# Copying a finished accumulator behind its last product, and wider planned spacing between engines, in a fused attention and feed-forward kernel

## Chip, core and metric

One core of one Trainium2 chip. The metric is the device time of one execution in microseconds (us), as a median over runs. The engines named below are TensorE (PE, its weight loads PEld), VectorE (DVE), ScalarE (ACT), GpSimd (POOL, here mostly an issuer of transfers) and SyncE (SP, the issuer of the other transfers). Each engine takes its instructions strictly in the order in which the program gives them to it.

## The reference

```python
# q, k, v: (4, 12480, 128); agents: (4, 49, 128); w_in: (128, 2048); w_out: (2048, 128)
def sm(a, b):
    s = scale * (a @ b.transpose(0, 2, 1))
    s = s - s.max(-1, keepdims=True)
    e = np.exp(s)
    return e / (e.sum(-1, keepdims=True) + 1e-09)
a2k = sm(agents, k)
agent_v = a2k @ v
q2a = sm(q, agents)
x = (q2a @ agent_v).reshape(49920, 128)
h = x @ w_in
g = np.maximum(h, 0.0) ** 2
out = g @ w_out
```

## The kernel before

The 49,920 rows are worked in 52 groups (`NSG`) of 960 rows (`ST`), 13 groups to each of the 4 batches. A group passes through 16 blocks (`NF`), one for each 128 columns of the 2048 wide hidden layer, so there are 832 blocks (`NG`). Products in float32 are made from a high part, rounded to the short format that TensorE takes, and a low part, the rest; each product is then three products.

A block `i` has these steps. `mm1(i)` (L493) makes 128 x 960 hidden values from the group's softmax rows `p_a` (high) and `p_b` (low) and the folded weights `w_a`, `w_b`: six matmuls, two at a time in the two halves of the array. `relu(i)` (L497) and `square(i)` (L500) run on ScalarE. `high(i)` rounds to `gh`, on VectorE (L507) for odd blocks and by a transfer issued from GpSimd (L505) for even ones. `low(i)` (L511) makes `gl` on VectorE. `mm2(i)` (L527) adds the block to the group's output, which fills the two accumulator banks `out0` and `out1`: twelve matmuls, eight blocks (`LAG`) behind `mm1`.

The two banks of `out` exist once (`ps_o`, `bufs=1`). When the last `mm2` of a group has run, `store_a` (L540) copies `out0` on ScalarE and `store_d` (L544) copies `out1` on VectorE into `ob`, and one transfer on SyncE's queue (L546) sends `ob` out. The first `mm2` of the next group overwrites the banks, and waits for both copies.

Beside that runs the attention work of later groups. For the softmax rows of a group the steps are `q_load`, `q_scores` (PE, L408), `q_turn` (DVE, L416), `q_shift` (DVE), `q_exp` (ACT, L432), `q_share` (DVE, from L436), `q_back` (DVE, L453), `q_spread` (eight small transfers on SyncE's queue, L461), `q_hi` (ACT, the cast that makes `p_a`, L465) and `q_lo` (DVE, which makes `p_b`, L468). The keys and values of the next batch are worked in similar chains (`k_pair`, `kp_copy`, `kp_max`, `k_exp`, `k_hi`, `v_hi`, `v_lo`, `v_acc`), which share one accumulator tile (`ps_att`, one buffer) with the query scores.

The order of everything is written by a planner. `at(t, f, ...)` files a step under a number `t` whose whole part is the block during which it is to run, a slot; all steps are sorted by `t` and issued in that order to their engines. In slot `i`, `mm2` of the pair that is due comes at `i`, `mm1(i)` at `i + .01`, `relu(i)` at `i + .1` (or `.035`), `square(i-1)` at `i + .2`, `low(i-4)` (odd) at `i + 0`, `low(i-5)` (even) at `i - .1`, `high(i-2)` at `i + .35`, and one step of the attention chains for each engine at `i + .5`. `chain` finds free slots for a chain: from a step on one engine to the next on another it leaves the number of slots in the table `hop`, and a bank's slots are held in `banks`. Slots of the copies are in `taken`, and the two or three slots up to them in `kept`, which only the steps in `urgent` may use.

The slot in which a group's last `mm2` runs is called T below: `T = s*16 + 23` for group `s`. There, `mm1(T)` and (by `early_mm1`, in all groups but the last three) `mm1(T+1)` are issued between the last `mm2` of the group and the first of the next, with `q_scores` of a later group ahead of them.

Of the kernel before, what the change touches and what calls it, by code (L numbers as in the profile page):

```python
# [9 lines left out]
F32 = mybir.dt.float32  # L10
# [7 lines left out]
P = 128  # L18
CH = 120
G = 8  # L20
TT = CH * G // 2
ST = CH * G
# [3 lines left out]
def agent_attention_relu2_kernel(ctx: ExitStack, tc: tile.TileContext, qT, kT, v, agT, w_in, w_out, outT):  # L26
# [6 lines left out]
    nc = tc.nc  # L33
    C, B, NCH, _ = kT.shape
# [11 lines left out]
    wk = ctx.enter_context(tc.tile_pool(name="wk", bufs=2))  # L46
# [424 lines left out]
    NSG = B * NS  # L471
# [3 lines left out]
    outs = {}  # L475
# [60 lines left out]
    obs = {}  # L536

    def store_a(s):
        obs[s] = wk.tile([P, 2, TT], F32, name="ob", bufs=1)
        nc.scalar.copy(obs[s][:, 0, :], outs[s][0][:, :TT])  # L540

    def store_d(s):
        ob = obs.pop(s)
        nc.vector.tensor_copy(ob[:, 1, :], outs.pop(s)[1][:, :TT])  # L544
        if s < NSG - 1:
            nc.sync.dma_start(out=outT[:, s * ST:(s + 1) * ST], in_=ob.rearrange("p t n -> p (t n)"))  # L546
        else:
            for t in range(2):
                nc.sync.dma_start(out=outT[:, s * ST + t * TT:s * ST + (t + 1) * TT], in_=ob[:, t, :])


    LAG = 8
    TAIL, EARLY = 52, 8
# [3 lines left out]
    def by_dma(i):  # L557
        return i % 2 == 0 and FROM <= i < NG - 4
# [4 lines left out]
    def at(t, f, *args):  # L563
        steps.append((t, len(steps), f, args))

    hop = {"PE": {"PE": 1, "PX": 0, "ACT": 0, "DVE": 0}, "PX": {"ACT": 0}, "ACT": {"PE": 2, "ACT": 1, "DVE": 0, "POOL": 3},
           "DVE": {"PE": 2, "ACT": 1, "DVE": 1, "POOL": 3}, "POOL": {"PE": 1, "ACT": 4, "DVE": 4, "POOL": 1}}
    taken = {(e, s * NF + NF - 1 + LAG) for s in range(NSG) for e in ("ACT", "DVE")}  # L570
    kept = {(e, s * NF + NF - 1 + LAG - x) for s in range(NSG) for e, n in (("ACT", 3), ("DVE", 2)) for x in range(n)}
    taken |= {("PE", s * NF + NF - 1 + LAG) for s in range(NSG - 3)}
# [2 lines left out]
    def chain(t, todo):  # L575

        first = prev = None
        while todo:  # L580
            n = 1
            while todo[0][0] == "PE" and n < len(todo) and (todo[n][1] in reads_bank and todo[n][0] != "PE" or todo[n][1:-1] == todo[n - 1][1:-1] and todo[n][1] is not k_max):
                n += 1
            t += hop[prev][todo[0][0]] if prev else 0
            while True:
                g, p, ts = t, None, []
                for e, f, *_ in todo[:n]:
                    g += hop[p][e] if p else 0
                    while (e, g) in taken or f not in urgent and (e, g) in kept:
                        g += 1  # L590
                    ts.append(g)
                    p = e
                held = range(ts[0], ts[-1] + (3 if todo[0][1] is v_acc else 2)) if todo[0][0] == "PE" else ()
                if not any(y in banks for y in held):
                    break
                t += 1
            banks.update(held)
            for (e, f, *args), g in zip(todo, ts):
                taken.add((e, g))
                at(g + (.005 + .015 * args[2] if f is w_make and args[2] < 2 else .5), f, *args)  # L600
            first = ts[0] if first is None else first
            prev, t, todo = p, ts[-1], todo[n:]
        return first, t
# [4 lines left out]
    def plan_queries(s):  # L608

        t = (s - 3) * NF + NF - 1 + LAG  # L610
        g = t + 1
        while ("DVE", g) in taken:
            g += 1
        banks.update(range(t, g + 2))
        taken.add(("DVE", g))
        at(t - 6, q_load, s)
        at(t + .005, q_scores, s)
        at(g + .5, q_turn, s)
        plan_rows(s, g + 1)

    def plan_rows(s, g):
        _, t = chain(g, [("DVE", q_shift, s), ("ACT", q_exp, s), ("DVE", q_share, s), ("DVE", q_back, s)])
        at(t + .9, q_spread, s)
        _, t = chain(t + 5, [("ACT", q_hi, s), ("DVE", q_lo, s)])
        assert t + 2 < s * NF, (s, t)

    def plan_queries_early(s, base):
        first, t = chain(base, [("PE", q_scores, s), ("DVE", q_turn, s)])
        plan_rows(s, t + 1)
        at(first - 6, q_load, s)  # L630
# [53 lines left out]
    order, t = {}, 6.3  # L684
# [37 lines left out]
    for n in range(NS):  # L722
        t = order["k", n] + 1.7
# [7 lines left out]
    for n in range(NS):  # L731
        t = t1 if n == 0 else max(t1 + .6 * n, order["v", n - 1] - .5) if n < S1 else t2 if n == S1 else order["v", n - 2] + .6
# [4 lines left out]
    t = order["q", 0] + .9  # L737
# [3 lines left out]
    for n in range(7):  # L741
        t = (10.3, 15.6, 27, 31.2, 35, 46, 52)[n]
# [5 lines left out]
    t = last  # L748
# [16 lines left out]
    at(3.08, q_scores, 1)  # L765
    at(4.04, q_turn, 1)
    banks.update([*range(5), *(x + y for x in SKIP for y in range(3))])
    plan_rows(1, 5)
    taken.update((e, t) for e in ("ACT", "DVE") for x in SKIP for t in (x, x + 1))
    for n in range(AHEAD, EARLY):  # L770
        at(3.55 + 2 * (n - AHEAD), k_load, 1, n)
# [16 lines left out]
    early_mm1 = {s * NF + NF + LAG + x: s * NF + NF - 1 + LAG + x + .02 for s in range(NSG - 3) for x in range(2)}  # L788
    for i in range(NG):
        late = i in SKIP or i < NF + LAG and (i < LAG or (i - LAG) % NF == 0)  # L790
        at(early_mm1.get(i, i if late else i + .01), mm1, i)
        at(i + (.035 if i + 1 in early_mm1 and i not in early_mm1 else .1), relu, i)
        at(i + 1.2, square, i)
        if i < FROM:
            at(i + 1.35, high, i)
            at(i + (2.32 if i <= SKIP[0] else 3.3), low, i)
        elif by_dma(i):
            at(i + 3.05, high, i)
            at(i + 4.9, low, i)
        else:  # L800
            at(i + 2.35, high, i)
            at(i + 4, low, i)
    for i in range(NF + LAG):
        j = i - LAG + sum(i <= x for x in SKIP)
        if j >= 0 and i not in SKIP:
# [5 lines left out]
                at(j + LAG + x + .001 * y, mm2, j + y, x ^ (j // 2 % 2), x + y + j % NF == 0, x + y == 2 and j % NF == NF - 2)  # L811
    for s in range(NSG - 1):
        t = s * NF + NF - 1 + LAG
        at(t + (.08 if t + 1 in early_mm1 else .15), store_a, s)
        at(t + .25, store_d, s)
    t, way = NG, (NG - LAG) // 2 % 2
    for js in (range(NG - LAG, NG - LAG // 2), range(NG - LAG // 2, NG)):
        for x in range(2):
            for j in js:
                at(t, mm2, j, way ^ x, False, x == 1 and j == NG - 1)  # L820
                t += 1
        way ^= 1
    at(t + .1, store_a, NSG - 1)
    at(t + .2, store_d, NSG - 1)
    with tc.manual_schedule():
        for _, _, f, args in sorted(steps, key=lambda x: x[:2]):
# [25 lines left out]
```

## Time and profile before

| | us |
|---|---|
| median of 3 runs | 1961.61 (1957.45 to 1962.17) |
| the profiled execution, its own time | 1961.79 |
| span of the profiled execution, first to last instruction | 1960.0 |
| TensorE busy (matmuls / weight loads) | 1847.1 / 1621.3 |
| ScalarE busy | 1663.2 |
| VectorE busy | 1598.2 |

The profiled execution's time lies within 0.2 us of the median, so sums made against its span can be read as sums against the median. Busy times of matmuls overlap, since one starts before the last has ended; where TensorE stood still is read from the starts of its instructions. An idle time is printed in brackets behind the instruction that ended it, with what it had waited for.

### The profile page before, as it was taken

What the parts mean: (1) busy time and instruction counts of PE and PEld (TensorE: products, weight loads), DVE (VectorE), ACT (ScalarE), POOL (GpSimd) and SP (SyncE); (2) the same over time, 40 slices, a digit from 0 to 9 for tenths busy, and PEclk for the clock granted to TensorE, in tenths of its full rate; (3) what the DMA queues carried; (4) which work ended last, traced back from release to release, by engine and by line L of the source; (5) the groups of instructions that cost most, each with busy time, mean ns of one, the idle gap of its engine ahead of it and who ended that gap; (6) DMA issues with size and microseconds to landing.
All of it is one profiled execution on the core that took longest, in us unless ns stands there. A gap on an engine that the chain in (4) does not pass through costs nothing.

```text
span 1960.0 us, 45341 instructions
## 1 busy us (share of the span) xinstructions
PE 1847.1 (94%) x18297; PEld 1621.3 (83%) x18297; DVE 1598.2 (82%) x2131; ACT 1663.2 (85%) x2015; POOL 325.3 (17%) x501
## 2 busy tenths in 40 slices
PE   9999999999999999999999999999999999999998
PEld 8688779888888887888887888877888788888887
DVE  6677888888888887888888888987887877888786
ACT  3578879888888988898888889987998898989897
POOL 0011122121111111122112213111111111111110
PEclk9999989999999999999999999999999999999999
DMA  9354544555444554554444454544444444444442
GB/s 342 121 169 143 197 155 163 190 184 186 155 156 168 167 185 168 170 192 156 164 170 141 168 168 166 179 158 148 163 157 146 143 159 151 158 161 157 161 148 102
DMA packets 110323, 325.19 MB, mean 166 GB/s; under 512 B 16672, under 2 KB 30368, under 8 KB 110112
## 3 DMA queue, kind: packets, MB, share of 16 engines
q0 software_dynamic: 58752, 200.57, 28.8%
q1 hardware_dynamic: 51360, 121.72, 18.8%
q8 instruction: 143, 2.34, 0.5%
q14 instruction: 68, 0.56, 0.1%
HBM read 83.35 MB, written 25.56 MB: 56 GB/s over the span
## 4 chain that ended last, share of the span: by engine, by line
PE 47%; DVE 20%; issue 10%; ACT 10%; DMA 8%; SPq 5%; ACTq 0%; DVEq 0%; POOLq 0%
PE out L527 27%; DVE gl L511 12%; PE h L493 12%; SPq L461 5%; DMA gh<-g 4%; ACT g L500 3%; DMA pt<-et 3%; ACT g L497 3%; DVE gh L507 3%; PE ps_att L192 3%; PE out L302 1%; PE ps_att L408 1%; PE ps_att L281 1%; DVE ob L544 1%; DVE sm L436 1%
## 5 line engine op out<-in xcount | busy, mean ns | idle before, releaser
L511 DVE TENSOR_TENSOR gl<-g,gh 128x960 fp32r<-128x960 f32 x832 | 934.5, 1158 | 100.3 <-PE out L527 69.8
L497 ACT ACTIVATE g<-h 128x960 f32<-128x960 f32 x832 | 814.0, 978 | 181.1 <-PE h L493 180.1
L500 ACT ACTIVATE g<-g 128x960 f32<-128x960 f32 x832 | 842.3, 1013 | 0.0
L527 PE MATMUL out<-gh,wo_hi 64*128 64x480 f32 x3328 | 728.8, 376 | 70.2 <-ACT ob L540 50.5
L527 PE MATMUL out<-gl,wo_hi 64*128 64x480 f32 x3328 | 713.6, 371 | 7.8 <-DVE gl L511 6.1
L527 PE MATMUL out<-gh,wo_lo 64*128 64x480 f32 x3328 | 711.8, 368 | 0.0
L527 PEld LDWEIGHTS out<-gh,wo_hi 64*128 64x128 f32 x3328 | 400.7, 188 | 121.2 <-ACT ob L540 69.6
L505 POOL DMA_DIRECT2D gh<-g x408 | 226.9, 556 | 1497.6 <-PE h L493 465.2
L527 PEld LDWEIGHTS out<-gl,wo_hi 64*128 64x128 f32 x3328 | 401.9, 188 | 49.5 <-DVE gl L511 26.6
L527 PEld LDWEIGHTS out<-gh,wo_lo 64*128 64x128 f32 x3328 | 404.7, 190 | 21.3
L493 PE MATMUL h<-p_a,w_a 49*128 49x480 f32 x1664 | 358.1, 382 | 16.5 <-ACT g L497 16.2
L493 PE MATMUL h<-p_a,w_b 49*128 49x480 f32 x1664 | 343.9, 365 | 0.0
L493 PE MATMUL h<-p_b,w_a 49*128 49x480 f32 x1664 | 343.8, 365 | 0.0
L507 DVE CAST gh<-g 128x960 fp32r<-128x960 f32 x424 | 285.4, 673 | 5.5 <-ACT g L500 4.7
L493 PEld LDWEIGHTS h<-p_a,w_a 49*128 49x128 f32 x1664 | 193.9, 188 | 59.0 <-ACT g L497 33.1
L493 PEld LDWEIGHTS h<-p_b,w_a 49*128 49x128 f32 x1664 | 195.8, 190 | 10.2
L493 PEld LDWEIGHTS h<-p_a,w_b 49*128 49x128 f32 x1664 | 192.2, 186 | 11.9
L468 DVE TENSOR_TENSOR p_b<-pt,p_a 113x480 fp32r<-113x480 f32 x52 | 34.3, 659 | 91.0 <-ACT p_a L465 82.6
L436 DVE TENSOR_REDUCE sm<-e 128x8 f32<-128x392 f32 x52 | 29.1, 560 | 95.7 <-ACT e L432 95.7
L251 POOL TENSOR_TENSOR sk<-sk,mM 120x196 f32<-120x196 f32 x78 | 91.8, 1187 | 15.9 <-PE ps_att L192 11.5
L192 PEld LDWEIGHTS ps_att<-ag_sb,kt 64*120 64x120 f32 x1248 | 77.1, 185 | 5.3 <-issue 2.8
L465 ACT CAST p_a<-pt 113x480 fp32r<-113x480 f32 x52 | 30.8, 593 | 57.2 <-DMA pt<-et 46.8
(127 smaller groups left out, 994.2 us busy)
## 6 DMA issues: line engine op xcount, KB each, us to landing
gh<-g POOLq DMA_DIRECT2D x408, 480.0 KB, 3.1
vt<-v SPq DMA_DIRECT2D x52, 516.0 KB, 5.4
qt<-qT SPq DMA_DIRECT2D x52, 488.0 KB, 4.4
kt<-kT SPq DMA_DIRECT2D x52, 480.0 KB, 5.8
outT<-ob SPq DMA_DIRECT2D x51, 480.0 KB, 2.6
pt<-et SPq DMA_DIRECT2D x416, 30.0 KB, 2.4
raw<-w_in SPq DMA_DIRECT2D x4, 512.0 KB, 7.8
raw<-w_out SPq DMA_DIRECT2D x4, 512.0 KB, 6.3
```

What stands on the lines that cost most here:

```text
L192: mm = nc.tensor.matmul(ps[:CH, u, r * A:(r + 1) * A], cols[u][r][rows], ag_sb[rows, b, :A], start=x == 0 and r == 0, stop=x == 1 and r == ...
L251: eng.tensor_tensor(out=x, in0=x, in1=m.rearrange("p (o a) -> p o a", o=1).to_broadcast([CH, G if h is None else H, A]), op=ALU.subtract)
L436: nc.vector.tensor_reduce(out=sms[s], in_=es[s][:, :, :A], axis=AX.X, op=ALU.add)
L461: nc.sync.dma_start(out=pts[s][to:to + 32, j % 2 * QW:(j % 2 + 1) * QW], in_=src[32 * j:32 * j + 32, h, :QW])
L468: nc.vector.tensor_tensor(PT[s][1][:M], pts.pop(s)[:M], PT[s][0][:M].bitcast(F32), op=ALU.subtract)
L493: nc.tensor.matmul(hs[i][:, t, :TT], w, two(p), start=n == 0, stop=n == 2)
L497: nc.scalar.activation(gs[i], hs.pop(i)[:, :, :TT], AF.Relu)
L500: nc.scalar.activation(gs[i], gs[i], AF.Square)
L505: nc.gpsimd.dma_start(out=ghs[i], in_=gs[i])
L507: nc.vector.tensor_copy(ghs[i], gs[i])
L511: nc.vector.tensor_tensor(out=gls[i], in0=gs.pop(i), in1=ghs[i].bitcast(F32), op=ALU.subtract)
L527: mm = nc.tensor.matmul(o[u][:, :TT], w[rows, j, :], two(g[rows, u, :]), start=first and n == 0, stop=last and n == 2)
```

## The change

The two copies of a group's output are issued directly behind its last `mm2`, at T + .003 and T + .004 (in the first group + .031 and + .032), where `store_a` stood at T + .08 (or .15), behind `relu(T)`, and `store_d` at T + .25. So that VectorE's copy comes first in its slot, `low` moves by .3 within its slot, behind the copy. Either copy may now be the first to make `ob`; the transfer is issued with the second. The table `hop` leaves one slot where it left none from ScalarE to VectorE, and two where it left one from VectorE to ScalarE. The casts of the softmax rows (`q_hi`, `q_lo`) are planned from 9 slots (4 for the groups 1 and 2) behind `q_back`, where it was 5.

```diff
     def store_a(s):
-        obs[s] = wk.tile([P, 2, TT], F32, name="ob", bufs=1)
-        nc.scalar.copy(obs[s][:, 0, :], outs[s][0][:, :TT])
+        nc.scalar.copy(ob_of(s)[:, 0, :], outs[s][0][:, :TT])
+        store(s)
 
     def store_d(s):
-        ob = obs.pop(s)
-        nc.vector.tensor_copy(ob[:, 1, :], outs.pop(s)[1][:, :TT])
-        if s < NSG - 1:
-            nc.sync.dma_start(out=outT[:, s * ST:(s + 1) * ST], in_=ob.rearrange("p t n -> p (t n)"))
-        else:
-            for t in range(2):
-                nc.sync.dma_start(out=outT[:, s * ST + t * TT:s * ST + (t + 1) * TT], in_=ob[:, t, :])
-
+        nc.vector.tensor_copy(ob_of(s)[:, 1, :], outs[s][1][:, :TT])
+        store(s)
+
+    def ob_of(s):
+        if s not in obs:
+            obs[s] = wk.tile([P, 2, TT], F32, name="ob", bufs=1)
+        return obs[s]
+
+    def store(s):
+        stored[s] = stored.get(s, 0) + 1
+        if stored[s] == 2:
+            ob = obs.pop(s)
+            outs.pop(s)
+            if s < NSG - 1:
+                nc.sync.dma_start(out=outT[:, s * ST:(s + 1) * ST], in_=ob.rearrange("p t n -> p (t n)"))
...
-    hop = {"PE": {"PE": 1, "PX": 0, "ACT": 0, "DVE": 0}, "PX": {"ACT": 0}, "ACT": {"PE": 2, "ACT": 1, "DVE": 0, "POOL": 3},
-           "DVE": {"PE": 2, "ACT": 1, "DVE": 1, "POOL": 3}, "POOL": {"PE": 1, "ACT": 4, "DVE": 4, "POOL": 1}}
+    hop = {"PE": {"PE": 1, "PX": 0, "ACT": 0, "DVE": 0}, "PX": {"ACT": 0}, "ACT": {"PE": 2, "ACT": 1, "DVE": 1, "POOL": 3},
+           "DVE": {"PE": 2, "ACT": 2, "DVE": 1, "POOL": 3}, "POOL": {"PE": 1, "ACT": 4, "DVE": 4, "POOL": 1}}
...
     def plan_rows(s, g):
         _, t = chain(g, [("DVE", q_shift, s), ("ACT", q_exp, s), ("DVE", q_share, s), ("DVE", q_back, s)])
         at(t + .9, q_spread, s)
-        _, t = chain(t + 5, [("ACT", q_hi, s), ("DVE", q_lo, s)])
+        _, t = chain(t + (9 if s > 2 else 4), [("ACT", q_hi, s), ("DVE", q_lo, s)])
...
-    plan_rows(1, 5)
+    plan_rows(1, 4)
...
         elif by_dma(i):
             at(i + 3.05, high, i)
-            at(i + 4.9, low, i)
+            at(i + 5.2, low, i)
         else:
             at(i + 2.35, high, i)
-            at(i + 4, low, i)
+            at(i + 4.3, low, i)
...
-        at(t + (.08 if t + 1 in early_mm1 else .15), store_a, s)
-        at(t + .25, store_d, s)
+        at(t + (.003 if s else .031), store_a, s)
+        at(t + (.004 if s else .032), store_d, s)
```

## Rows read from the trace of the kernel before

**Rows 1.** The page, part 1: busy us, share of the span, instructions

```profile
PE 1847.1 (94%) x18297; PEld 1621.3 (83%) x18297; DVE 1598.2 (82%) x2131; ACT 1663.2 (85%) x2015; POOL 325.3 (17%) x501
```

**Rows 2.** Waits, whole span: who waited for whom, us, times, longest us

```profile
ACT g L497 <- PE h L493: 180.1, 187, 3.2
...
DVE sm L436 <- ACT e L432: 95.7, 49, 2.8
DVE p_b L468 <- ACT p_a L465: 82.6, 43, 4.6
...
PE out L527 <- ACT ob L540: 50.5, 51, 2.4
ACT p_a L465 <- DMA pt<-et: 46.8, 21, 4.4
...
PE out L527 <- DVE ob L544: 16.5, 20, 1.6
PE h L493 <- ACT g L497: 16.2, 19, 2.3
```

**Rows 3.** Timeline of PE around a group's end: start us, us, line, op, tiles

```profile
959.31 0.37 PE L527 MATMUL out<-gl,wo_hi 64*128 64x480 f32 x2
959.61 1.07 PE L408 MATMUL ps_att<-qt,ag_sb 128*32 128x256 f32 x16
...
961.52 0.36 PE L493 MATMUL h<-p_b,w_a 49*128 49x480 f32 x2
961.73 0.37 PE L493 MATMUL h<-p_a,w_b 49*128 49x480 f32 x2
963.00 0.52 PE L527 MATMUL out<-gh,wo_hi 64*128 64x480 f32 x2 [0.91 <-ACT ob L540]
```

**Rows 4.** Timeline of ACT, the same group's end

```profile
959.37 0.99 ACT L500 ACTIVATE g<-g 128x960 f32<-128x960 f32 x1
961.53 0.97 ACT L497 ACTIVATE g<-h 128x960 f32<-128x960 f32 x1 [1.16 <-PE h L493]
962.39 0.55 ACT L540 COPY ob<-out 128x480 f32<-128x480 f32 x1
```

**Rows 5.** Timeline of DVE, a group's end at which DVE is late

```profile
402.54 2.21 DVE L511 TENSOR_TENSOR gl<-g,gh 128x960 fp32r<-128x960 f32 x2
404.67 0.65 DVE L544 COPY ob<-out 128x480 f32<-128x480 f32 x1
```

**Rows 6.** Timeline of PE, that same group's end

```profile
399.59 0.37 PE L527 MATMUL out<-gl,wo_hi 64*128 64x480 f32 x2
...
405.37 0.47 PE L527 MATMUL out<-gh,wo_hi 64*128 64x480 f32 x1 [1.63 <-DVE ob L544]
```

**Rows 7.** Timeline of PE, end of one of the last three groups

```profile
1898.93 0.47 PE L527 MATMUL out<-gh,wo_hi 64*128 64x480 f32 x2 [2.45 <-ACT ob L540]
```

**Rows 8.** Timeline of SP, eight transfers that one `q_spread` issues

```profile
975.50 5.69 SPq L461 DMA_DIRECT2D pt<-et  x8
```

**Rows 9.** The page, part 6: transfers by line, KB each, us to landing

```profile
pt<-et SPq DMA_DIRECT2D x416, 30.0 KB, 2.4
```

**Rows 10.** Timeline of ACT in the last batch, around the cast

```profile
1684.93 1.00 ACT L500 ACTIVATE g<-g 128x960 f32<-128x960 f32 x1
1688.01 0.59 ACT L465 CAST p_a<-pt 113x480 fp32r<-113x480 f32 x1 [2.08 <-DMA pt<-et]
1688.51 0.96 ACT L497 ACTIVATE g<-h 128x960 f32<-128x960 f32 x1
```

**Rows 11.** Timeline of PE just behind that cast

```profile
1689.52 0.47 PE L493 MATMUL h<-p_a,w_a 49*128 49x480 f32 x2 [0.63 <-ACT g L497]
```

**Rows 12.** Windows, last batch: length, busy PE, PEld, DVE, ACT, POOL, PEclk, DMA

```profile
1500.00:1930.00 430.00, 403.19 (x3913) 354.68 (x3911) 344.34 (x435) 385.55 (x454) 57.09 (x104) 1.00 0.44 154
```

**Rows 13.** Waits in 1510 to 1895 us, eleven groups' ends

```profile
ACT p_a L465 <- DMA pt<-et: 22.3, 9, 3.8
...
PE h L493 <- ACT g L497: 11.4, 11, 2.3
```

**Rows 14.** All of L540's copies: ns min/median/max, first and last start

```profile
L540 ACT COPY ob<-out x52: 551/552/612, 133.8 to 1955.5; 128x480 f32<-128x480 f32 x52
```

More of the change, by code (lines that the diff above doesn't have):

```diff
@@ L538, in store_a @@
     def store_a(s):
-        obs[s] = wk.tile([P, 2, TT], F32, name="ob", bufs=1)
-        nc.scalar.copy(obs[s][:, 0, :], outs[s][0][:, :TT])
+        nc.scalar.copy(ob_of(s)[:, 0, :], outs[s][0][:, :TT])
+        store(s)
     def store_d(s):
-        ob = obs.pop(s)
-        nc.vector.tensor_copy(ob[:, 1, :], outs.pop(s)[1][:, :TT])
-        if s < NSG - 1:
-            nc.sync.dma_start(out=outT[:, s * ST:(s + 1) * ST], in_=ob.rearrange("p t n -> p (t n)"))
-        else:
-            for t in range(2):
-                nc.sync.dma_start(out=outT[:, s * ST + t * TT:s * ST + (t + 1) * TT], in_=ob[:, t, :])
+        nc.vector.tensor_copy(ob_of(s)[:, 1, :], outs[s][1][:, :TT])
[11 more added lines that the diff above has]
+                nc.sync.dma_start(out=outT[:, s * ST:(s + 1) * ST], in_=ob.rearrange("p t n -> p (t n)"))
+            else:
+                for t in range(2):
+                    nc.sync.dma_start(out=outT[:, s * ST + t * TT:s * ST + (t + 1) * TT], in_=ob[:, t, :])
+    stored = {}
     LAG = 8
```

## Prediction

> **What bounds the kernel now.** First the page's busy times: PE 94%, ScalarE 85%, VectorE 82% [rows 1]. Three engines lie close together, and TensorE is the fullest, so I ask what TensorE waits for and then whether the other two could keep up if it waited less.
>
> The same line shows weight loads busy for 83%. Matmuls of 0.37 us start every 0.20 us [rows 3], so the 94% count some time twice. The Trainium skill ("Perfetto Trace Analysis", Identifying the Most-Contended Engine) says that the matmul busy share is a bad measure of how near TensorE is to its limit and that the share of the weight loads is a better one. By the first share 113 us of the span are idle, and the gross gain worked out below would be two thirds of it; by the second 339 us are idle, which leaves room for the rival in which more comes back.
>
> The second view is therefore the list of waits over the span, with starts, not busy times, for what a wait costs. TensorE waits 50.5 us in 51 waits for ScalarE's copy of a finished output and 16.5 us in 20 waits for VectorE's, 67.0 us in 71 waits; its next largest wait for an engine is 16.2 us for `relu` [rows 2]. One group's end shows the mechanism. The last `mm2` starts at 959.31, `q_scores` and two `mm1` follow, and the last `mm1` pair starts at 961.73, 0.20 us after the one before it. The next pair was due at 961.93 and starts at 963.00 [rows 3]: 1.07 us lost, of which 0.91 are printed as idle, since the matmul before is still in flight for 0.37 us. ScalarE meanwhile was done with `square` at 960.36, stood idle for 1.16 us until `mm1(T)` had run, did `relu(T)`, and only then copied a bank that had been complete since 959.7: copy from 962.39 to 962.94, TensorE 0.06 us later [rows 3, 4]. The copy stands behind the wrong wait.
>
> The other two engines have waits of their own. VectorE waits 95.7 us for `q_exp` and 82.6 us for `q_hi`; ScalarE waits 46.8 us for the spread softmax rows [rows 2].
>
> **The change, part by part.** *Copies first.* With the copy ahead of `relu(T)`, ScalarE in the group shown is free at 960.36, copies until 960.9, and its `relu(T)` still starts at 961.53, when `mm1(T)` is done. VectorE copies from about the same time for 0.65 us [rows 4, 5]. Both are done a microsecond before 961.93, so `q_scores` and two `mm1` hide them. Without that cover (the last groups have one `mm1` and no `q_scores`) the copy would stand open: 0.37 for the matmul, 0.65 for the copy, 0.06 to restart, 1.08 us against some 0.8 of cover, about 0.3 us a group, where today 2.45 us are idle [rows 3, 5, 7].
>
> What it frees: 67.0 us of idle, and per wait the 0.16 us by which the loss by starts exceeds the printed idle, 71 x 0.16 = 11 us. Gross 78 us.
>
> What stays: VectorE is sometimes late. In the group at 399.59 it starts two `low` at 402.54 and copies at 404.67, so TensorE goes on at 405.37 [rows 5, 6]. With the copy ahead of the two `low` it runs from 402.54 to 403.19 and TensorE could go on at 403.25; by the pattern of rows 3 it is ready 2.62 us after its last `mm2` start, at 402.21. So 1.0 us remains there. For the 20 waits of this sort I take 0.4 us each as estimate, between nothing and 1.0: 8 us (bounds 0 to 20). Net for this part 70 us.
>
> The two `low` that now stand behind the copy are 2.2 us of work [rows 5]. `low(T-5)` could run earlier before; now it waits for the last `mm2`. It is needed at T+3, so nothing is put down (worked out under the rivals).
>
> *The casts later.* `q_back` falls on T+4 in the old table, and T+6 in the new one. `q_spread` holds SyncE's queue for 5.69 us for its eight transfers, and each lands 2.4 us after its issue [rows 8, 9]: about 8.1 us, 3.6 slots at the pace of 35.7 us for 16 blocks, (1955.5 - 133.8) / 51 [rows 14]. VectorE runs ahead or behind by a slot or two, and with five slots ScalarE often arrives first. In the last batch it stands 2.08 us before the cast, and behind that TensorE stands 0.63 us before `mm1` for the `relu` that came late [rows 10, 11]. Nine slots from T+6 lead into ScalarE's kept slots T+14 to T+16, so the cast falls on T+17, its partner on T+18; the rows are needed at T+25, seven slots or 15 us later. The wait of 46.8 us on ScalarE goes. TensorE's share of it is the 16.2 us for `relu` plus 19 x 0.16 = 3 us; 11.4 of the 16.2 lie in the last batch, in 11 waits for 11 groups, beside 22.3 us of waits for the spread rows there [rows 2, 13]. I take 15 of the 19 us (bounds 5 to 19: the `relu` could be late for other reasons).
>
> *Wider hops.* One slot more between `q_exp` and `q_share`, `q_hi` and `q_lo`, `v_hi` and `v_lo`, and so on, is worth about a slot, 2.2 us; VectorE's waits are 95.7 / 49 = 2.0 and 82.6 / 43 = 1.9 us each [rows 2], so nearly all of these 178 us of VectorE idle should go. TensorE does not wait there, it only feels a VectorE that is late: I put 5 us to it (0 to 25, the upper end the late copies and late `low` together). The chains get two or three slots longer and `ps_att` is held a slot longer for each of some 20 key chains; were TensorE idle in each such slot that would be 20 x 2.2 = 44 us, but in program order it has its blocks to do there. Taken at nothing, since the planner has free slots in which to put the work; the bound goes into the range. The output's transfer moves with the copy, so SyncE reaches it and all behind it sooner; `q_spread` moves two slots later and may hold back loads behind it on that queue, which have six to eight slots, over 13 us, of lead. Nothing.
>
> *Given back.* ScalarE is nearly the bound itself. In the last batch it is busy 385.55 of 430 us [rows 12], so a group of 33 us holds 29.6 us of its work. If a group loses 1.07 us at its end and 1 us at the cast it takes 31, and ScalarE is at 95%. Some of TensorE's spared time must come back as waits for `relu`. I take 10 us, half of all TensorE now loses that way (bounds 0 to 40, half of what is saved).
>
> Sum: 70 + 15 + 5 - 10 = 80 us off the profiled execution's 1961.8 us, which lies within 0.2 us of the median of the runs, 1961.6. That gives 1882 us, 4.1% less.
>
> **The rivals.** *Given back* (1905 to 1950, say 1925): the copies leave TensorE's path, but ScalarE and VectorE at 85% and 82% become the bound and TensorE waits for `relu` or `gl` inside the group. For it: ScalarE at 90% in the last batch already [rows 12]. Against: ScalarE waits 180.1 us for `mm1` [rows 2], so it has time that a faster TensorE hands it. Half of 85 us comes back: 1920, more with the held slots.
>
> *More comes back* (under 1845, say 1840): with VectorE freed of 178 us of waits, `low`, the late copies and `relu` are all on time. The gross 78, the 19 and the 25 us without loss give 122 us: 1840. Against: ScalarE would stand at 90% of the whole span.
>
> *VectorE's queue blocks* (slower). The copy at the head of slot T waits for the last `mm2`, and two `low` and all behind them wait with it. In the late group they would end at 402.54 + 0.65 + 2.2 = 405.4. TensorE needs them at T+3: behind 0.3 and 1.0 us for `q_scores`, 21 pairs at 0.20 us (two `mm1`, an `mm2`, an `mm1`, an `mm2`) and the 1.0 us still lost there, at 406.1 [rows 3, 5, 6]. That leaves 0.7 us even there. For the whole kernel to get slower each of the 51 group ends would have to lose more than the 1.6 us that it saves (80 us over 51), so VectorE would have to be 2.3 us later, at the average group, than in that late one. That gives 1970 to 1990; what VectorE is freed of speaks against it.
>
> *No change*: the copies are hidden and the groups' pace is set by something else, 1962. Against it stands that TensorE's own start is printed as released by the copy, 71 times [rows 2].
>
> **How the numbers follow.** My forecast (1845 to 1905) has 0.62; given back 0.20; more comes back 0.07; no change 0.04; slower 0.07. This kernel's runs can tell about 0.3% from no change. Faster: 0.62 + 0.20 + 0.07 = 0.89; same 0.04; slower 0.07. The range reaches from 1840, the sum without losses, to 1928, which takes in two thirds of the rival that gives back; that is 0.62 + 0.13 + 0.04, about 0.8. Predicted: 1882 us.
>
> **What would show it.** The waits of TensorE for the two copies fall from 67.0 us to under 12; ScalarE's copy starts within 1.1 us of the last `mm2` and ahead of `relu(T)`; the wait for the spread rows is under 5 us, and VectorE's waits for `q_exp` and `p_a` fall from 178 to under 30. The groups' pace falls from 35.7 to about 34.2 us. If TensorE's waits for `relu` exceed 40 us or those for `gl` 30 us, the gain was given back; if a copy still ends a wait in most groups, the cover was misjudged. A wait for a cast `p_a` or `p_b` at a group's first `mm1` would show that the casts are now too late.

## The result, and the profile after

The changed kernel takes 1829.6 us (median of 4 runs, 1827.3 to 1830.2) against 1961.9 us for the kernel before (1957.5 to 1967.6): ratio 0.932, 95% interval 0.930 to 0.935. It is 132 us faster, where 80 were forecast, and lies below the stated range. The direction was right and so was the place; the size was not, by 52 us.

The page of the changed kernel, part 1, against [rows 1]: the busy times of VectorE and ScalarE are the same within 9 us, and they now fill 88% and 91% of a shorter span.

```profile
PE 1791.2 (98%) x18297; PEld 1616.6 (88%) x18297; DVE 1602.4 (88%) x2131; ACT 1654.8 (91%) x2015; POOL 320.3 (18%) x501
```

The waits of the changed kernel over its span, against [rows 2]. TensorE's wait for ScalarE's copy, VectorE's for `q_exp` and TensorE's for `relu` no longer stand in the list's upper part. What is left of the copies is mostly VectorE's, 10 waits; ScalarE's end 5 waits, 2.5 us. One wait is new in size: VectorE before `low`, for the transfers that make `gh`, 30.0 us in the kernel before.

```profile
ACT g L497 <- PE h L493: 107.2, 131, 4.9
DVE gl L511 <- DMA gh<-g: 104.6, 68, 5.3
...
PE out L527 <- DVE ob L543: 12.7, 10, 2.5
```

One group's end after the change: timelines of TensorE, ScalarE and VectorE, against [rows 3, 4, 5].

```profile
945.41 0.37 PE L527 MATMUL out<-gl,wo_hi 64*128 64x480 f32 x2
945.71 1.07 PE L408 MATMUL ps_att<-qt,ag_sb 128*32 128x256 f32 x16
...
947.62 0.36 PE L493 MATMUL h<-p_b,w_a 49*128 49x480 f32 x2
947.83 0.37 PE L493 MATMUL h<-p_a,w_b 49*128 49x480 f32 x2
948.03 0.37 PE L527 MATMUL out<-gh,wo_hi 64*128 64x480 f32 x2
```

```profile
945.47 0.99 ACT L500 ACTIVATE g<-g 128x960 f32<-128x960 f32 x1
946.36 0.55 ACT L539 COPY ob<-out 128x480 f32<-128x480 f32 x1
947.62 0.97 ACT L497 ACTIVATE g<-h 128x960 f32<-128x960 f32 x1 [0.71 <-PE h L493]
```

```profile
945.85 0.66 DVE L543 COPY ob<-out 128x480 f32<-128x480 f32 x1 [0.58 <-PE out L527]
946.42 2.22 DVE L511 TENSOR_TENSOR gl<-g,gh 128x960 fp32r<-128x960 f32 x2
```

The last `mm2` starts at 945.41 as it did at 959.31, the same work follows, and the next `mm2` starts 0.20 us behind the last `mm1` pair, not 1.27. ScalarE copies 0.95 us after the last `mm2` start, inside the time in which it stood idle before, and `relu(T)` waits for `mm1(T)` as it did. The copies cost nothing here.

**An account by starts.** The idle times that a view prints miss part of what a wait costs, so for the table below every matmul from 140 us on was taken whose start lies more than 0.04 us beyond the usual distance from the one before it (0.20 us behind a 480 wide pair, about 0.12 behind the others). What exceeds that distance is filed under what ended the wait; where nothing is named it counts as the lower clock if the granted clock was then at the lower of its two levels (1.2 GHz in place of 2.4), and otherwise as a restart. The columns behind `after` are versions told in the experiments below: copies alone, copies and hops, copies and casts, `low` not shifted, `low` of even blocks later. Times in us; the profiled executions' times stand in the last line.

| TensorE's lost time | before | after | copies_only | copies_hops | copies_casts | low_unshifted | low_even_later |
|---|---|---|---|---|---|---|---|
| waits for the two copies | 79.0 | 17.8 | 11.8 | 22.9 | 6.8 | 59.6 | 3.5 |
| at the lower clock | 26.6 | 4.9 | 8.4 | 6.7 | 0.0 | 24.2 | 0.0 |
| waits for `relu`, `square` | 21.7 | 2.4 | 23.9 | 4.2 | 0.7 | 1.2 | 0.8 |
| waits for `gl`, `gh` | 15.8 | 2.6 | 17.6 | 0.9 | 29.8 | 4.1 | 10.8 |
| inside and around `q_scores` | 23.9 | 24.0 | 24.1 | 23.2 | 24.8 | 24.3 | 25.0 |
| restarts and the rest | 39.6 | 27.0 | 42.1 | 21.6 | 63.6 | 27.7 | 25.2 |
| sum | 206.6 | 78.7 | 127.8 | 79.6 | 125.8 | 141.1 | 65.3 |
| profiled time | 1961.8 | 1830.2 | 1878.1 | 1830.7 | 1874.5 | 1901.3 | 1813.0 |

From before to after the sum falls by 127.9 us and the profiled time by 131.6: TensorE's own losses are nearly all of the gain. 61 of it is the copies, 22 the clock, 19 `relu`, 13 `gl`, 13 the rest.

The line on the clock is seen behind one group's end of the kernel before. Windows of that kernel around the group's end at 771 us, at which both copies were waited for (the number behind POOL is the granted clock, 1.00 for 2.4 GHz and 0.50 for 1.2):

```profile
765.00:771.00 6.00, 4.67 (x47) 2.90 (x44) 5.05 (x7) 6.00 (x9) 0.53 (x1) 1.00 0.39 140
772.00:778.00 6.00, 5.42 (x28) 4.62 (x30) 2.97 (x5) 3.32 (x5) 0.53 (x1) 0.50 0.63 228
```

### The profile page after: what moved, and what is told of

Read it like the earlier page. It is cut to its first block, busy times and chain, and to the rows that moved or that the text cites. A ratio compares the mean times of both kernels' runs of the same rounds, so it can differ in the third digit from the quotient of the medians.

```text
span 1828.4 us, 45336 instructions
## 1 busy us (share of the span) xinstructions
PE 1791.2 (98%) x18297; PEld 1616.6 (88%) x18297; DVE 1602.4 (88%) x2131; ACT 1654.8 (91%) x2015; POOL 320.3 (18%) x501
## 4 chain that ended last, share of the span: by engine, by line
PE 70%; DVE 10%; ACT 8%; DMA 7%; issue 5%; DVEq 0%; POOLq 0%; ACTq 0%; SPq 0%
PE out L527 40%; PE h L493 20%; DMA gh<-g 6%; DVE gl L511 5%; ACT g L497 4%; ACT g L500 3%; PE ps_att L192 3%; PE ps_att L408 2%; DVE gh L507 2%; PE ps_att L281 1%; PE out L302 1%; PE h L181 1%; PE out L688 1%; PE ps_att L380 0%; PE ps_one L181 0%
## 5 line engine op out<-in xcount | busy, mean ns | idle before, releaser
L511 DVE TENSOR_TENSOR gl<-g,gh 128x960 fp32r<-128x960 f32 x832 | 937.1, 1165 | 118.3 <-DMA gh<-g 104.6
L527 PE MATMUL out<-gh,wo_hi 64*128 64x480 f32 x3328 | 679.8, 369 | 19.7 <-DVE ob L543 12.7
L527 PE MATMUL out<-gl,wo_hi 64*128 64x480 f32 x3328 | 667.2, 364 | 1.5 <-DVE gl L511 1.5
L527 PE MATMUL out<-gh,wo_lo 64*128 64x480 f32 x3328 | 667.6, 363 | 0.0
L527 PEld LDWEIGHTS out<-gh,wo_hi 64*128 64x128 f32 x3328 | 365.2, 186 | 53.1 <-DVE ob L543 17.3
L527 PEld LDWEIGHTS out<-gl,wo_hi 64*128 64x128 f32 x3328 | 366.9, 186 | 24.3 <-DVE gl L511 3.5
L527 PEld LDWEIGHTS out<-gh,wo_lo 64*128 64x128 f32 x3328 | 368.6, 187 | 19.6
L493 PE MATMUL h<-p_a,w_a 49*128 49x480 f32 x1664 | 340.5, 377 | 1.2 <-ACT g L497 1.1
L192 PE MATMUL ps_att<-ag_sb,kt 64*120 64x49 f32 x1248 | 74.6, 266 | 3.0 <-issue 3.0
L543 DVE COPY ob<-out 128x480 f32<-128x480 f32 x52 | 33.9, 653 | 27.6 <-PE out L527 27.6
L408 PE MATMUL ps_att<-qt,ag_sb 128*32 128x256 f32 x816 | 54.6, 385 | 0.0
```

The costliest lines, as they stand in the source:

```text
L192: mm = nc.tensor.matmul(ps[:CH, u, r * A:(r + 1) * A], cols[u][r][rows], ag_sb[rows, b, :A], start=x == 0 and r == 0, stop=x == 1 and r == ...
L408: nc.tensor.matmul(ps[32 * j:32 * j + 32, h * QB:(h + 1) * QB], ag_sb[:, s // NS, 32 * h:32 * h + 32], qt[:, j * QW:j * QW + QB], start=Tr ...
L493: nc.tensor.matmul(hs[i][:, t, :TT], w, two(p), start=n == 0, stop=n == 2)
L511: nc.vector.tensor_tensor(out=gls[i], in0=gs.pop(i), in1=ghs[i].bitcast(F32), op=ALU.subtract)
L527: mm = nc.tensor.matmul(o[u][:, :TT], w[rows, j, :], two(g[rows, u, :]), start=first and n == 0, stop=last and n == 2)
L543: nc.vector.tensor_copy(ob_of(s)[:, 1, :], outs[s][1][:, :TT])
```

## The experiments

The theory after the result: the parts add up, each by the losses that it takes away. The rival: the wider hops carry the gain, or at least what the forecast missed.

**Copies alone** (the changed kernel with copies and `low` as they are there, and the table `hop` and the casts as in the kernel before).

```diff
-    hop = {"PE": {"PE": 1, "PX": 0, "ACT": 0, "DVE": 0}, "PX": {"ACT": 0}, "ACT": {"PE": 2, "ACT": 1, "DVE": 1, "POOL": 3},
-           "DVE": {"PE": 2, "ACT": 2, "DVE": 1, "POOL": 3}, "POOL": {"PE": 1, "ACT": 4, "DVE": 4, "POOL": 1}}
+    hop = {"PE": {"PE": 1, "PX": 0, "ACT": 0, "DVE": 0}, "PX": {"ACT": 0}, "ACT": {"PE": 2, "ACT": 1, "DVE": 0, "POOL": 3},
+           "DVE": {"PE": 2, "ACT": 1, "DVE": 1, "POOL": 3}, "POOL": {"PE": 1, "ACT": 4, "DVE": 4, "POOL": 1}}
...
-        _, t = chain(t + (9 if s > 2 else 4), [("ACT", q_hi, s), ("DVE", q_lo, s)])
+        _, t = chain(t + 5, [("ACT", q_hi, s), ("DVE", q_lo, s)])
...
-    plan_rows(1, 4)
+    plan_rows(1, 5)
```

> The kernel before with the copies directly behind the last product and low shifted, but with the old hops and the old place of the casts. Theory (the parts add up: copies about 61 us of waits, and with them most of the 22 us lost at the lower granted clock behind long waits and some restarts): about 1875 us, waits of TensorE for copies under 25 us, stretches at the lower clock fewer than half of the 12 inside the run of the kernel before. Rival (the wider hops are what lets the copies pay, since VectorE and ScalarE would give the time back): 1915 us or more, with waits for relu or gl over 50 us.

Measured 1872.4 us, ratio 0.956 (0.954 to 0.958): 85 us off, and no sign of the rival. The trace has 3 stretches at the lower clock behind 140 us where before it had 13. The waits of this kernel that did not go:

```profile
DVE p_b L468 <- ACT p_a L465: 77.9, 40, 4.5
DVE sm L436 <- ACT e L432: 70.6, 49, 2.9
ACT p_a L465 <- DMA pt<-et: 55.0, 25, 4.4
...
PE h L493 <- ACT g L497: 17.8, 21, 2.4
```

**Casts alone**, on the kernel before.

```diff
-        _, t = chain(t + 5, [("ACT", q_hi, s), ("DVE", q_lo, s)])
+        _, t = chain(t + (9 if s > 2 else 5), [("ACT", q_hi, s), ("DVE", q_lo, s)])
```

> The kernel before with only the casts planned nine slots behind q_back in place of five (groups 1 and 2 as before). Theory: the waits of TensorE for relu, 22 us by starts, go nearly to nothing and the rest stays: about 1938 us. Rival (ScalarE's time is used up at the group's end): under 10 us gained.

Measured 1919.6 us, ratio 0.981 (0.977 to 0.984): 38 us, twice the theory's. `relu` is no longer waited for, as the theory had it (21.7 to 0.2 us in the same account), and most of the rest is the clock: 26.6 to 6.2 us, with 3 stretches at the lower level. The copies' waits hardly changed; ScalarE's copy still ends 51 of TensorE's waits, 47.2 us.

**Hops alone**, on the kernel before: the two lines of the table as in the changed kernel, and the casts of groups 1 and 2 a slot nearer, so that they fit.

```diff
-        _, t = chain(t + 5, [("ACT", q_hi, s), ("DVE", q_lo, s)])
+        _, t = chain(t + (5 if s > 2 else 4), [("ACT", q_hi, s), ("DVE", q_lo, s)])
...
-    plan_rows(1, 5)
+    plan_rows(1, 4)
```

> The kernel before with only the wider hop table (and the first two groups' casts a slot or so nearer, so that they fit). Theory: VectorE's waits for q_exp and p_a fall from 178 us to under 40, and TensorE gains only what it lost to gl and to late VectorE copies, 15 to 30 us: about 1940 us. Rival (the hops are the main part): 1905 us or less.

Measured 1926.8 us, ratio 0.982 (0.978 to 0.986): 30 us. But the wait of ScalarE for the spread rows went too, with the casts as near as ever, as the waits of this kernel show; and VectorE's copy became later than before [rows 2]. The clock fell with that: the trace has 16 stretches at the lower level that begin behind 140 us, against 13, and the mean granted clock of the four runs is 0.973 to 0.981, where the runs of the kernel before beside them have 0.980 to 0.985. Part of what the hops gave was so lost again.

```profile
PE out L527 <- ACT ob L540: 48.6, 51, 1.6
...
PE out L527 <- DVE ob L544: 33.4, 17, 3.6
DVE sm L436 <- ACT e L432: 30.5, 33, 1.8
...
ACT p_a L465 <- DMA pt<-et: 6.6, 4, 4.4
```

**Hops and casts without the copies** (the changed kernel, `store_a`, `store_d` and `low` at their old numbers).

```diff
-            at(i + 5.2, low, i)
+            at(i + 4.9, low, i)
...
-            at(i + 4.3, low, i)
+            at(i + 4, low, i)
...
-        at(t + (.003 if s else .031), store_a, s)
-        at(t + (.004 if s else .032), store_d, s)
+        at(t + (.08 if t + 1 in early_mm1 else .15), store_a, s)
+        at(t + .25, store_d, s)
```

> The changed kernel with the copies and low at their old places: hops and casts alone. Theory (parts add up): 1905 to 1915 us, waits for ScalarE's copy again about 50 us, a handful of stretches at the lower clock. Rival (hops and casts carry the gain): 1875 us or less.

Measured 1920.7 us, ratio 0.981 (0.978 to 0.983): 37 us for the two together, where they gave 38 and 30 alone. They do not add up. So the theory needs one correction: hops and casts cure the same wait.

**Copies and hops, without the later casts** (the changed kernel).

```diff
-        _, t = chain(t + (9 if s > 2 else 4), [("ACT", q_hi, s), ("DVE", q_lo, s)])
+        _, t = chain(t + (5 if s > 2 else 4), [("ACT", q_hi, s), ("DVE", q_lo, s)])
```

> The changed kernel with the casts again planned five slots behind q_back: copies and hops without the later casts. With hops alone ScalarE's wait for the spread rows had already fallen to 6.6 us. Theory (wider hops and later casts cure the same wait): 1828 to 1838 us, waits of TensorE for relu under 6 us. Rival (the casts have their own share, as in the run with casts alone): 1850 us or more.

Measured 1830.3 us, ratio 0.933 (0.929 to 0.937): the same as the changed kernel. The later casts add nothing once the hops are wide. The reason can be read from the two lines that bound the transfer: from the end of `q_back` on VectorE to the moment at which ScalarE is ready for the cast, the median over 49 groups is 6.5 us in the kernel before, 6.5 with copies alone, 8.1 with copies and hops, 8.4 with hops alone, for some 8.1 us of issue and landing [rows 8, 9]. VectorE, which no longer stands before `q_share`, is that much earlier at `q_back`.

**Copies and casts, without the hops** (the changed kernel with the old table `hop`).

```diff
-        _, t = chain(t + (9 if s > 2 else 4), [("ACT", q_hi, s), ("DVE", q_lo, s)])
+        _, t = chain(t + (9 if s > 2 else 5), [("ACT", q_hi, s), ("DVE", q_lo, s)])
...
-    plan_rows(1, 4)
+    plan_rows(1, 5)
```

> The changed kernel with the old hop table: copies and later casts without wider hops (groups 1 and 2 as before). Theory (the casts take away the 24 us that TensorE waited for relu with copies alone; the 18 us for gl stay): 1845 to 1855 us. Rival (gains of single parts add up, 1957 less 85 and 38): 1834 us or less.

Measured 1876.7 us, ratio 0.957 (0.953 to 0.961): no gain over copies alone, and 22 us worse than the theory. `relu` is no longer waited for, but VectorE, with no slot between `q_hi` and `q_lo`, waits 104.1 us for the cast, which now lies just behind a group's end. Waits of this kernel:

```profile
DVE p_b L468 <- ACT p_a L465: 104.1, 48, 5.0
...
PE out L527 <- DVE gl L511: 20.3, 54, 1.5
...
PE ps_att L281 <- DVE e L416: 14.2, 15, 1.3
```

`q_turn`, `low` and all behind that wait are late, and TensorE waits for these in place of `relu`.

**Low not shifted** (the changed kernel).

```diff
-            at(i + 5.2, low, i)
+            at(i + 4.9, low, i)
...
-            at(i + 4.3, low, i)
+            at(i + 4, low, i)
```

> The changed kernel with low at its old numbers (i + 4.9 and i + 4), so that VectorE's copy comes behind the two low of its slot, while ScalarE's copy stays first. Theory (the order on VectorE matters, two low are 2.2 us and the cover is 2.2 us at most): TensorE waits 35 to 60 us for VectorE's copy, the granted clock falls below 0.985, and the time is 1860 to 1885 us. Rival (VectorE is early enough now, it has lost its waits): within 6 us of the changed kernel's 1830.

Measured 1899.9 us, ratio 0.967 (0.965 to 0.970): 70 us slower than the changed kernel, more than the theory said. At this group's end VectorE first waits for a transfer, then does four `low`, and copies 6.7 us after the last `mm2`; TensorE, here with the last `mm2` at 400.66, starts the second bank 4.37 us late. Timelines of VectorE and TensorE:

```profile
401.32 2.72 DVE L511 TENSOR_TENSOR gl<-g,gh 128x960 fp32r<-128x960 f32 x2 [3.75 <-DMA gh<-g]
403.97 1.02 DVE L507 CAST gh<-g 128x960 fp32r<-128x960 f32 x1
404.91 0.35 DVE L258 CAST pe<-sk 120x392 fp32r<-120x392 f32 x1
405.18 2.21 DVE L511 TENSOR_TENSOR gl<-g,gh 128x960 fp32r<-128x960 f32 x2
407.32 0.64 DVE L543 COPY ob<-out 128x480 f32<-128x480 f32 x1
```

```profile
408.02 0.76 PE L527 MATMUL out<-gh,wo_hi 64*128 64x480 f32 x1 [4.37 <-DVE ob L543]
```

Behind it the granted clock drops. Windows of this kernel just before and behind that wait (the number behind POOL is the clock):

```profile
395.00:401.00 6.00, 6.00 (x64) 5.41 (x62) 2.58 (x4) 6.00 (x8) 0.61 (x2) 1.00 1.07 379
408.00:415.00 7.00, 6.98 (x40) 6.00 (x42) 3.97 (x6) 1.86 (x2) 0.57 (x1) 0.56 0.64 218
```

In the first TensorE runs at 2.4 GHz, in the second mostly at 1.2: 40 matmuls fall in its 7 us, against 64 in 6. The Trainium skill ("TensorE: Matmul & The Clock Gate", Part 1) says that the array's clock is gated by how busy it has lately been, and falls to half when it idles. The trace agrees: of the 13 such stretches of the kernel before, 61 us in all behind its start, 12 lie behind a group's end at which both copies were waited for, and one behind a `relu` that came 2.5 us late. It also shows that such a wait need not be followed by one: there are 20 ends with both waits, and 8 of them have no such stretch.

**More work in the gap** (the kernel before; five more pairs of products at the head of `mm1(T+1)`, whose result the real products overwrite).

```diff
         hs[i] = new_h()
+        if i in filled:
+            for t in [0, 1] * 5:
+                rows = slice(64 * t, 64 * t + A)
+                nc.tensor.matmul(hs[i][:, t, :TT], wa[rows, f], two(pa[rows]), start=True, stop=True)
...
+    filled = {s * NF + NF + 8 for s in range(1, NSG - 3)}
```

> The kernel before with five more pairs of products at each group's end (49 of them, their result overwritten), about 1.0 us of TensorE work in the 1.07 us and more in which it waits for the copies; the copies stay where they are. Theory (standing still is what brings the lower clock): stretches at the lower clock fall from 12 to 4 or fewer, the time lost in them from 27 us to under 10, and the kernel gets about 15 us faster, 1942 us, though it does more. Rival (the lower clock comes from something else): 12 stretches as before and 1957 to 1965 us.

Measured 1947.3 us, ratio 0.993 (0.990 to 0.995): faster by 13 us with 48 us more work for TensorE: the edit fills 48 group ends, not 49, and the trace has 480 matmuls more. The mean granted clock rises from 0.982 to 0.989 over the runs, 0.7% of 1960, 14 us, which is about the gain. The count was missed: 9 stretches at the lower clock remain, not 4. The waits for ScalarE's copy nearly go, 50.5 us before, but five pairs fill 1.0 us and the waits for VectorE's copy, 16.5 us before, go on behind them:

```profile
PE out L531 <- DVE ob L549: 16.9, 20, 2.0
...
PE out L531 <- ACT ob L545: 6.2, 9, 2.4
```

That less idle time at the groups' ends means less time at the lower clock is borne out, in direction and in the time gained; that a 1.0 us fill would prevent it was wrong.

**The transfers for `gh` a slot earlier** (the changed kernel).

```diff
-            at(i + 3.05, high, i)
+            at(i + 2.05, high, i)
```

> The changed kernel with the transfers that make gh for even blocks issued a slot earlier (high at i + 2.05 in place of 3.05). Theory (the VectorE copies that are still late, 15 us of waits at 10 group ends, are late because VectorE stood before low for such a transfer, 105 us in all): the copies' waits fall under 8 us and the kernel comes to 1812 to 1822 us. Rival (the transfers are late because of the other loads, or GpSimd's queue then holds up TensorE): 1828 us or more.

Measured 2013.3 us, ratio 1.027 (1.022 to 1.032): slower than the kernel before. The copies' waits do vanish (0.5 us by starts), but the rival's wait is far larger. GpSimd's queue also holds the empty instructions that pass a bank from one half of the array to the other in `mm2` (`relay`, L522); at i + 2.05 the transfer waits for `square` ahead of the next of them. Waits of this kernel:

```profile
POOL gh L505 <- ACT g L500: 1029.6, 263, 5.8
PEld out L527 <- POOLq L522: 260.7, 354, 1.7
...
PE out L527 <- POOLq L522: 140.7, 282, 1.3
```

**The later copies' cause.** In the changed kernel a late group looks like this (VectorE, then TensorE): a wait for a transfer of `gh`, two `low`, `high`, a step of the keys, the copy.

```profile
240.87 2.23 DVE L511 TENSOR_TENSOR gl<-g,gh 128x960 fp32r<-128x960 f32 x2 [2.92 <-DMA gh<-g]
243.01 0.65 DVE L507 CAST gh<-g 128x960 fp32r<-128x960 f32 x1
243.58 0.56 DVE L261 TENSOR_TENSOR pe<-sk,pe 120x392 fp32r<-120x392 f32 x1
244.06 0.65 DVE L543 COPY ob<-out 128x480 f32<-128x480 f32 x1
```

```profile
244.76 0.47 PE L527 MATMUL out<-gh,wo_hi 64*128 64x480 f32 x1 [2.31 <-DVE ob L543]
```

**Low of even blocks a slot later** (the changed kernel).

```diff
-            at(i + 5.2, low, i)
+            at(i + 6.2, low, i)
```

> The changed kernel with low of even blocks a slot later (i + 6.2 in place of 5.2), behind the transfer that makes its gh, which so has a slot more. Theory (the copies still late are late because VectorE stood before low for that transfer, 105 us in all): that wait falls under 40 us, the waits for copies under 8 us, and the time to 1808 to 1820 us. Rival (low is then too late for mm2): waits of TensorE for gl over 20 us, 1830 us or more.

Measured 1813.3 us (1811.6 to 1813.7), ratio 0.923 (0.921 to 0.925). This beats both kernels, the changed one by 16 us. VectorE hardly waits for the transfers any more, no stretch at the lower clock is left, and a little is paid in waits for `gl`. Waits of this kernel:

```profile
DVE gl L511 <- DMA gh<-g: 9.9, 9, 3.5
...
PE out L527 <- DVE gl L511: 8.4, 12, 1.4
```

**Queries loaded earlier** (the changed kernel).

```diff
-        at(t - 6, q_load, s)
+        at(t - 10, q_load, s)
```

> The changed kernel with the load of a group's queries filed ten slots ahead of the group's end in place of six. Theory (the transfers of gh that make VectorE late just there are slow because this load runs beside them): VectorE's waits for gh fall by a third and the time to 1815 to 1825 us. Rival (the slow transfers come from the keys and values): no change, 1827 to 1833 us.

Measured 1823.4 us, ratio 0.929 (0.926 to 0.931). VectorE's wait for `gh` falls from 104.6 to 77.6 us, by a quarter and not by the third expected, the copies' waits from 17.8 to 6.7 us. The median is 6 us under the changed kernel's, but the intervals of the two ratios overlap, so the gain itself is likely and not shown.

**Both of the last two edits.**

> Both of the last two edits together. Theory: no more than the later low alone, within 5 us of it, since what it hides cannot be gained twice. Rival: another 8 us or more.

Measured 1811.8 us, ratio 0.923 (0.921 to 0.924): the same as the later `low` alone, as the theory said.

## Why the forecast was too small

*Copies first.* The mechanism was right, and the group shown went as worked out: copies in ScalarE's idle time, TensorE on at 0.20 us. The term was 70 us; the waits for the copies fell by 61 in the changed kernel and by 67 with copies alone. But copies alone gave 85 us, and taken out of the changed kernel, together with the shift of `low`, they cost 91 (1829.6 to 1920.7). What the step left out is the clock: 12 of 20 group ends at which both copies were waited for are followed by stretches at 1.2 GHz, 26.6 us of lost time in the kernel before, 8.4 with copies alone. The prediction looked at no granted clock at all, although the page and the windows have a column for it. Its remark that the copies' residue would be VectorE's lateness held, 15.2 of the 17.8 us, but that is twice the 8 us it set aside.

*Low behind the copy.* Put down at nothing as a cost, which was right; the 2.2 us it gives VectorE's copy were weighed only for the 20 late waits. In the changed kernel it carries 70 us, 42 of them in waits for the copies and 19 at the lower clock: without it the two `low`, and the waits for transfers that now fall on them, stand ahead of the copy.

*Casts later.* 15 us. TensorE's waits for `relu` went as forecast (21.7 to 2.4), and the later casts alone do that (0.2); but with wide hops they go with the casts at five slots too (4.2). Measured on top of copies and hops: nothing, 1830.3 against 1829.6.

*Wider hops.* This is the step that failed: "TensorE does not wait there, it only feels a VectorE that is late: I put 5 us to it". On top of the copies they are worth 42 us by the medians (1872.4 to 1830.3; beside them the kernel before took 1957.2 and 1960.5) and 47 by the profiled executions: 20 of `relu`, 17 of `gl`, 20 of restarts and the rest, 3 of the clock and `q_scores`, less 11 of later copies. What makes up the 20 of restarts and the rest is not resolved: some 9 are short late starts of `mm1` for which the trace names no cause. VectorE's 178 us of waits went, as forecast (32 us are left with copies and hops, 5 in the changed kernel), and that VectorE was then early enough to set `q_back`, `low` and `q_turn` on time was taken for the lesser effect. The upper bound given for this term, 25 us, was too low as well, since it took from the waits TensorE has for VectorE by name and not from those that VectorE passes on through ScalarE. These, the 20 of `relu`, the prediction had priced under the casts; casts and hops together were put at 20 us and gave 43 on top of the copies (1872.4 to 1829.6). The two entries of the table that changed were not run apart.

*Given back.* 10 us were set aside because ScalarE would be full. Nothing came back: ScalarE is busy 389.97 of 400 us in the last batch now, and the list of waits of that stretch has none of TensorE for `relu`. Window of the changed kernel, against [rows 12]:

```profile
1400.00:1800.00 400.00, 398.20 (x3964) 362.97 (x3962) 348.31 (x440) 389.97 (x459) 55.47 (x104) 1.00 0.49 167
```

The sum by what was measured, in this order of adding the parts: 85 for copies with the shifted `low`, where 70 was forecast, 42 for hops (5), 0 for casts (15), 0 given back (10), 127 of the 132 us. *The rivals:* "more comes back" was the right one, and its 1840 us, the sum with no loss, still lacked the clock. Against it stood that ScalarE would be at 90% of the span; it is at 91%, and that is no objection. By the account, which starts at 140 us, TensorE lost 207 us in the kernel before and 79 in the changed one. The share of the matmuls leaves 113 and 37 us idle, that of the weight loads 339 and 212: the first is too small and the second too large, and the first is the nearer in both kernels. The Trainium skill ("Perfetto Trace Analysis", Identifying the Most-Contended Engine) prefers the second; here the starts decide, and neither share gives the loss. VectorE's queue did not block: VectorE stands 27.6 us before its copies, where it was 3.4, but the two `low` behind the copy are done in time, and TensorE's waits for `gl` and `gh` fell from 15.8 to 2.6 us. The wait for casts at a group's start did not appear. Of the signs set beforehand, the groups' pace fell to 33.1 us, (1823.9 - 137.2) / 51 by ScalarE's copies, where 34.2 was forecast, and the copies' printed waits to 15.2, where under 12 was.

*What stays open.* The trace shows 3 stretches at the lower clock with the casts alone and none with copies and casts, although the first still waits for copies at every group's end; hops alone, with the same waits for ScalarE's copy and more for VectorE's, has 16. Which idle times bring the lower clock and which do not is not told apart by these runs.

## What to carry to other kernels

When an accumulator that exists once is copied out by two engines, put both copies first in their engines' queues at that point and see what stands ahead of each: the copy that is late decides, and its engine's own waits come with it. In an in-order schedule a wait that costs its own engine only idle time is still worth removing when that engine feeds a third, because the lateness is passed on and shows under another name. Parts of a change that cure the same wait must be tried together and apart before either is given a price.

## What was not expected of the hardware

Runs of one kernel differ by the granted clock. Of 24 runs of the kernel before whose clock is recorded, the fastest, 1953.2 us, has a mean granted clock of 0.985 and the slowest, 1972.9 us, of 0.977: 19.7 us, where 0.8% of the span is 15.7. The changed kernel's four runs lie at 0.992 to 0.993 within 2.9 us, and those of the version with the later `low`, with no lower stretch in its profile, within 2.1 us. What goes with the spread is the clock and not the waiting as such: the version with the transfers a slot earlier has TensorE wait 140.7 us for GpSimd, in 282 waits of at most 1.3 us, and its four runs have 0.995 to 0.996 and lie within 2.7 us.

Transfers of the same 480 KB that make `gh` land 3.2 us after their issue in the median, and at three of the late group ends `low` followed 4.3 to 5.0 us after it. At the one of 240 us loads of a query, a value and two key tiles had been issued within the 5 us ahead of it, and with the query load moved VectorE's waits for such transfers fell by a quarter. That these loads are what slows the transfers is therefore likely and not shown.
